# Three edits to a fused sparse-attention and expert kernel: the gate's weight by a transfer, one joint set of block sums, an uneven last output

## The chip, the cores and the metric

The kernel runs on one core of a Trainium2 chip. The metric is device time in microseconds of one execution; the time before is the median of three runs, 151.57 us (151.08 to 153.88). A trace from the hardware profiler covers one further execution.

## What is computed

Four batches, 8 heads, 768 positions, head size 64. Each query attends to keys less than 16 positions away and to 24 block summaries of its head (the maximum of 32 keys, the mean of 32 values, plus log 32 on the score). The heads side by side give `x` of 768 x 512 per batch. The mean of `x` over the positions times a 512 x 8 matrix picks one of 8 experts per batch and a weight, and that expert's two products follow.

```python
scores = concat([where(|i - j| < 16, q k^T / 8, -1e9), q k_sum^T / 8 + log(32)])
x = softmax(scores) @ concat([v, v_sum])              # 4 x 768 x 512
logits = x.mean(positions) @ w_gate                   # 4 x 8
e, g = argmax(logits), max(softmax(logits))           # one expert and one weight per batch
out[b] = g * (relu(x[b] @ w1[e]) @ w2[e])             # 512 -> 1024 -> 512
```

## The kernel before, in words

Work is tiled by batch `b` (0 to 3), by pair of heads `pr` (0 to 3) and by parity `u` of the 64-query tile. For a pair, TensorE (PE) turns the keys (`tk`, L555) and the queries (`tq`, L602); VectorE (DVE) and ScalarE (ACT) move them out of PSUM (`ke` and `ko`, two window copies of the keys; `eq` for the queries; all at L412 or L414), DVE takes the maximum per block of keys (`kmw`, L579) and ACT copies it in beside the windows (`kb`, L588). Then come the scores (`qk`, L624; in batch 0 with two products of a mask more, L634), the exponential on ACT (`ex`, L643 or L646), a mask on DVE (`mk`, L652, batches 1 to 3), the product with the values (`av`, L671 and L682), the division on DVE (`nm`, L694 and L695), a transpose (`tx`, L708) and a copy to `xT` on ACT, which also sums over the positions (`xc`, L716).

The values need block sums (`v_ops`): products of the values with a 0/1 matrix. For batches 0 and 1 each half of the heads has a set of 7 products over all 128 output rows (`half`, L435). For batches 2 and 3 one set of 14 products does both halves, each product using 64 columns of the array at its own place (`joint`, L461). Their results are copied by `ev` and spread to the tiles `vb` and `vo` by DVE (`sums`, L490; `odd`, L509 and L511).

The gate of a batch (`gate`): `lgf` (L857), four fp32 products of the sums with `w_gate`; `mxf` (L864 to L869), the maximum and its index on DVE; `ldf`, GpSimd (POOL) reads the index into a register and sends for the chosen expert's weights, `w1` (L882; for batch 0 in three parts of 256, 256 and 512 columns) and `w2` (L888). On the side, `exf` (ACT, L895) and `rcf` (DVE, L902) make the weight g in one element; `gpf` (PE, L905) multiplies it with a row of ones, which brings it to 128 partitions of a PSUM bank, and `gcf` (DVE, L912) copies that to `gcol`. In batch 0 the last pair's sum comes from `pxf` (PE, L843) and `pcf` (DVE, L849).

The expert (`moe`): `h` (L960), products with `w1` into one PSUM bank each, 12 groups a batch, with `rl` (ACT L971 or DVE L973) after each; then six row blocks `o_st` (L996, 8 products of 512 columns), `ev` (ACT L1005 or DVE L1007), which scales by `gcol`, and an output transfer on SyncE's (SP's) queue (L1013). An output tile is one of 7 buffers. The last block of the last batch is made in two pieces of 256 columns.

Nothing is reordered while it runs. Each piece of work is added once with a number, and `ORDER` (L21) is the order in which all are issued; `ENGINE` says which of DVE or ACT does a copy; `FILL` puts idle products (L1152, 128 x 512, results unused) ahead of a numbered piece on PE. Each engine's queue takes its pieces in that order and waits at the first that isn't ready. POOL's queue, in order: the loads of q, k, v of batches 0 and 1; gate 0's `w1`, half of batch 2's q and k, `w2`, the rest of batch 2; gate 1's `w1`, batch 3's loads with `w2` of batch 1 between them; then `w1`, `w2` of gates 2 and 3. PSUM holds one double bank (`pair`), five single banks and the two banks of `kps` for turned keys. Setup work of DVE (masks, memsets; `setup_far`, L282, `setup_bind`, L304) is in the same order.

The three stages the text speaks of: the start (0 to 30 us, batch 0's attention, ended by gate 0), the middle (30 to 90 us, attention of batches 1 and 2 mixed with the experts of 0 and 1) and the end (batch 3's attention, the experts of 2 and 3).

Of the kernel before, what the change touches and what calls it, by code (L numbers as in the profile page):

```python
# [10 lines left out]
FP32 = mybir.dt.float32  # L11
# [4 lines left out]
ACT = mybir.ActivationFunctionType  # L16
# [2 lines left out]


ORDER = [  # L21
    2, 5, 4, 21, 23, 25, 0, 1, 3, 8, 6, 11, 12, 13, 7, 22, 24, 34, 14, 35, 36, 41, 9, 10, 39,
    29, 27, 46, 42, 37, 40, 38, 55, 47, 15, 43, 56, 44, 45, 57, 30, 61, 16, 26, 17, 28, 18,
    19, 20, 31, 48, 58, 32, 59, 33, 49, 62, 60, 50, 63, 65, 51, 53, 69, 74, 54, 75, 76, 77,
    66, 52, 70, 71, 72, 78, 80, 82, 86, 79, 88, 73, 106, 83, 87, 92, 90, 93, 64, 96, 67, 89,
    94, 137, 100, 97, 81, 91, 95, 68, 138, 102, 107, 108, 139, 84, 98, 101, 85, 147, 103, 112,
    99, 142, 148, 149, 140, 113, 109, 114, 130, 115, 125, 121, 143, 141, 164, 152, 110, 111,
    116, 117, 118, 119, 122, 123, 144, 126, 165, 166, 154, 150, 124, 104, 145, 183, 129, 169,
    167, 153, 131, 151, 159, 155, 168, 170, 188, 127, 160, 171, 178, 189, 105, 146, 132, 128,
    157, 325, 134, 172, 179, 321, 213, 156, 214, 326, 161, 162, 176, 190, 184, 329, 173, 163,  # L30
    323, 158, 177, 322, 185, 330, 327, 133, 333, 191, 324, 135, 174, 343, 335, 186, 334, 181,
    180, 238, 192, 136, 175, 344, 195, 328, 187, 197, 202, 336, 337, 182, 198, 239, 203, 199,
    196, 341, 342, 339, 204, 240, 338, 248, 200, 120, 340, 201, 243, 207, 209, 253, 244, 208,
    205, 210, 254, 206, 331, 193, 241, 211, 194, 212, 249, 332, 345, 219, 242, 215, 250, 346,
    245, 220, 255, 348, 224, 246, 216, 351, 251, 265, 225, 252, 226, 256, 349, 231, 230, 257,
    266, 267, 260, 272, 227, 247, 352, 268, 261, 273, 354, 217, 218, 284, 270, 269, 289, 221,
    228, 271, 285, 290, 229, 232, 237, 279, 280, 355, 286, 357, 358, 360, 361, 222, 468, 262,
    474, 469, 475, 314, 234, 315, 316, 317, 223, 274, 235, 233, 318, 319, 460, 458, 258, 236,
    263, 461, 277, 282, 459, 382, 387, 291, 287, 288, 264, 259, 383, 278, 384, 388, 281, 292,
    320, 480, 466, 481, 467, 283, 298, 303, 299, 304, 392, 296, 393, 478, 464, 385, 479, 465,  # L40
    472, 473, 275, 297, 476, 394, 300, 470, 386, 477, 471, 276, 305, 293, 301, 395, 409, 308,
    310, 374, 302, 311, 389, 390, 391, 462, 306, 309, 350, 347, 359, 410, 307, 294, 411, 375,
    295, 482, 356, 312, 463, 485, 483, 313, 363, 353, 412, 413, 364, 486, 397, 414, 398, 428,
    415, 396, 372, 373, 433, 368, 399, 404, 434, 369, 488, 400, 405, 376, 377, 379, 406, 370,
    371, 429, 430, 401, 489, 416, 423, 417, 418, 424, 431, 491, 402, 407, 492, 408, 403, 421,
    426, 422, 435, 494, 436, 425, 432, 442, 447, 443, 448, 497, 378, 427, 495, 365, 419, 420,
    366, 367, 438, 439, 381, 437, 527, 380, 515, 509, 517, 498, 449, 444, 516, 510, 528, 518,
    440, 445, 446, 452, 454, 455, 523, 529, 524, 525, 441, 493, 450, 453, 456, 511, 451, 530,
    531, 457, 500, 512, 521, 526, 532, 496, 487, 362, 519, 484, 501, 505, 522, 490, 520, 502,
    513, 499, 533, 534, 536, 537, 514, 539, 542, 506, 507, 545, 508, 548, 540, 543, 503, 571,  # L50
    504, 572, 567, 546, 568, 538, 569, 563, 564, 559, 549, 565, 557, 566, 558, 560, 553, 573,
    574, 554, 570, 551, 561, 555, 552, 556, 575, 578, 541, 581, 562, 576, 535, 547, 579, 550,
    580, 544, 584, 582, 583, 585, 586, 577, 587, 590, 588, 591, 589, 593, 594, 592, 595,
]

ENGINE = {
    7: "DVE", 8: "ACT", 9: "ACT", 10: "DVE", 31: "ACT", 35: "DVE", 36: "ACT", 40: "DVE", 42:
    "ACT", 43: "ACT", 47: "DVE", 49: "DVE", 50: "ACT", 54: "DVE", 70: "ACT", 71: "ACT", 75:
    "DVE", 87: "DVE", 126: "ACT", 128: "ACT", 138: "ACT", 139: "ACT", 143: "DVE", 148: "ACT",
    149: "ACT", 153: "DVE", 165: "ACT", 166: "ACT", 170: "DVE", 184: "ACT", 185: "ACT", 189:  # L60
    "DVE", 229: "DVE", 239: "DVE", 240: "ACT", 244: "ACT", 249: "DVE", 250: "ACT", 254: "ACT",
    266: "ACT", 267: "ACT", 271: "ACT", 285: "DVE", 286: "ACT", 290: "DVE", 322: "ACT", 324:
    "ACT", 326: "ACT", 328: "DVE", 330: "ACT", 332: "DVE", 334: "ACT", 336: "ACT", 338: "ACT",
    340: "ACT", 342: "DVE", 344: "ACT", 346: "ACT", 349: "ACT", 352: "DVE", 355: "ACT", 358:
    "ACT", 361: "ACT", 373: "ACT", 383: "ACT", 384: "ACT", 388: "DVE", 393: "DVE", 394: "ACT",
    398: "ACT", 410: "ACT", 411: "DVE", 415: "DVE", 429: "ACT", 430: "ACT", 434: "DVE", 459:
    "ACT", 461: "ACT", 463: "DVE", 465: "ACT", 467: "ACT", 469: "ACT", 471: "ACT", 473: "ACT",
    475: "ACT", 477: "ACT", 479: "ACT", 481: "ACT", 483: "ACT", 486: "DVE", 489: "DVE", 492:
    "ACT", 495: "ACT", 498: "ACT", 510: "ACT", 512: "ACT", 514: "ACT", 516: "ACT", 518: "ACT",
    520: "DVE", 522: "ACT", 524: "ACT", 526: "DVE", 528: "DVE", 530: "DVE", 532: "ACT", 534:  # L70
    "DVE", 537: "ACT", 540: "DVE", 543: "ACT", 546: "DVE", 549: "DVE", 552: "DVE", 554: "DVE",
    556: "DVE", 558: "ACT", 560: "DVE", 562: "DVE", 564: "ACT", 566: "DVE", 568: "DVE", 570:
    "ACT", 572: "DVE", 574: "ACT", 576: "DVE", 579: "ACT", 582: "ACT", 585: "ACT", 588: "DVE",
    591: "ACT", 594: "ACT",
}

FILL = {
    34: 11, 41: 6, 46: 2, 55: 1, 98: 1, 104: 1, 144: 1, 154: 1, 164: 1,
}


# [79 lines left out]
def kernel(  # L161
# [10 lines left out]
    nc = tc.nc  # L172

    B, H, S, D = q.shape
    E = moe_w_gate.shape[1]
    DM = H * D
# [12 lines left out]
    NST = S // 128  # L189
# [3 lines left out]
    SP = S // G  # L193
# [12 lines left out]
    const_pool = ctx.enter_context(tc.tile_pool(name="const", bufs=1))  # L206
# [36 lines left out]

    BIND = 4 * (NT - 1)
    bind = const_pool.tile([128, BIND + 128], BF16, name="bind")
    ones_row = const_pool.tile([1, 128], FP32, name="ones_row")

# [64 lines left out]
            nc.vector.memset(kps.bitcast(FP32)[:, :, a // 2 : (a + PADA) // 2], 0.0)  # L314

    def setup_kw():
        nc.vector.memset(ones_row, 1.0)
        for t in kws:
            nc.vector.memset(t[:, :, :, KW + NB : 128], 0.0)

# [68 lines left out]
        nc.gpsimd.dma_start(wg_sb, moe_w_gate.rearrange("(g p) e -> p g e", p=128))  # L389

    sch = Sched(len(single))
    JOINT = 2
    add = sch.add
    state = {}
    last_T, last_av = {}, {}
# [439 lines left out]
    def gate(b, att, w_deps, order, between=None):  # L835
        sb = state[b]
        _, x_ops, x_sums = att
        last = by_pe(b, NP - 1)
# [62 lines left out]
            sb["grec"] = sm_pool.tile([1, 1], FP32, name="grec")  # L901
            nc.vector.reciprocal(sb["grec"], sb["se"])  # L902

        def gpf():
            nc.tensor.matmul(  # L905
                sb["lgps"][:, E : E + 1], lhsT=ones_row[0:1, :], rhs=sb["grec"][0:1, 0:1],
                start=True, stop=True,
            )

        def gcf():  # L910
            sb["gcol"] = sm_pool.tile([128, 1], FP32, name="gcol", bufs=B)
            nc.vector.tensor_copy(sb["gcol"], sb["lgps"][:, E : E + 1])  # L912

        if last:
            o_px = add("PE", 0.35, x_sums, pxf, num=12, shape="w", take=1)
            o_pc = add("DVE", 0.16, [o_px, x_ops[0]], pcf)
            o_lg = add("PE", 0.2, x_ops[:-1] + [o_pc, wg_load], lgf, num=8, shape="w")
        else:
            o_px = o_lg = add("PE", 0.2, x_ops + [wg_load], lgf, num=8, shape="w", take=1)
        o_mx = add("DVE", 0.67, [o_lg], mxf)  # L920
        o_ld = add("POOL", 1.5, [o_mx] + w_deps, ldf, after=order)
        w1s, prev, c0 = [], [o_ld], 0
        for c1 in W1_PARTS[b]:
# [8 lines left out]
        w2 = add("POOL", 0.9, [], w2f, dma=6.2, count=1, after=prev)  # L932
        o_ex = add("ACT", 0.3, [o_mx], exf)
        o_rc = add("DVE", 0.15, [o_ex], rcf)
        o_gp = add("PE", 0.3, [o_rc, kw_set], gpf, num=2, shape="g")
        o_gc = add("DVE", 0.16, [o_gp], gcf, give=[o_px])
        return w1s, w2, o_gc

    EVICT = 20.0
# [1 line left out]
    def moe(b, w, att):  # L941
        w1s, w2, o_gc = w
        sb = state[b]
# [92 lines left out]
        hsl["first"] = firsts[0]  # L1036
        last = [o_st(st) for st in range(NST - (b == B - 1))]
        if b == B - 1:
            last += [o_st(NST - 1, 0, DM // 2), o_st(NST - 1, DM // 2, DM)]
        return last  # L1040


# [84 lines left out]
    order = load_batch(1, order)  # L1127
    sch.prio = 60.0
    gates[0] = gate(0, att[0], [], order)
    order = [gates[0][2]]  # L1130
    att[1] = attend(1, 30.0)
    order = load_batch(2, order)
    sch.prio = 30.0
    gates[1] = gate(1, att[1], [], order)
    order = [gates[1][2]]
    for b in range(B):
        if b + 2 < B:
            att[b + 2] = attend(b + 2, 10.0)
            if b + 3 < B:
                sch.prio = 0.0  # L1140
                order = load_batch(b + 3, order)
        sch.prio = 0.0
        moe_last[b] = moe(b, gates[b], att[b])
        if b + 2 < B:
            sch.prio = 10.0
            gates[b + 2] = gate(b + 2, att[b + 2], moe_last[b], order)
            order = [gates[b + 2][2]]

    def fill(i, n):

# [37 lines left out]
```

## Time and profile before

| | |
|---|---|
| median of 3 runs | 151.57 us |
| the profiled execution, its own time | 152.49 us |
| span of its trace | 150.7 us |
| busy: PE, DVE, ACT, POOL | 141.6, 103.8, 94.0, 35.2 us |
| mean granted TensorE clock | 0.989 |
| software DMA queue (POOL's): moved, share of 16 engines' span | 17.50 MB, 94.3% |
| hardware DMA queue (SP's): moved, share | 7.08 MB, 13.3% |

Times in the trace count from the start of the span; 1.8 us of the execution lie outside it. In a timeline row stand start, length, engine, line, operation, output and inputs, count, and in brackets the idle time before it with what ended it ("issue" is idle time for which the profile shows no wait). In the slices each digit is a fortieth of the span (3.77 us) in tenths. Of a transfer the trace gives the time from issue to landing.

### The profile page before, as it was taken

The numbers are of one execution on the slowest core, as the hardware profiler recorded it, in microseconds if no ns is written. First come the engines' busy times: TensorE is split into PE (matmuls) and PEld (weight loads), VectorE is DVE, ScalarE is ACT, GpSimd is POOL, SyncE is SP. The second block draws the span as 40 slices with busy tenths as digits, with TensorE's granted clock in tenths as the row PEclk, the third lists the DMA queues.
The fourth block names the chain that finished last, engine by engine and source line by source line (L and its number), as shares of the span: only waits on it lengthen the run. The fifth ranks groups of instructions, "written<-read, shape, count | busy, mean of one in ns | idle before, by whom it ended". The sixth has DMA issues, their size and how long they took to land.

```text
span 150.7 us, 4728 instructions
## 1 busy us (share of the span) xinstructions
PE 141.6 (94%) x2005; PEld 87.4 (58%) x2023; DVE 103.8 (69%) x244; ACT 94.0 (62%) x185; POOL 35.2 (23%) x44
## 2 busy tenths in 40 slices
PE   6988989799999999999899999999999999999990
PEld 2356758567657665566564857555576445465460
DVE  5988987569999889589579978999453222556010
ACT  3277877769968899776788978969563310140331
POOL 7959500039900004942000005000004000000000
PEclk9999999879999999999999999999999999999999
DMA  4999999919999999999999991999931999910353
GB/s 147 190 171 185 190 177 195 123 11 146 166 207 202 174 197 118 145 246 218 251 215 207 192 71 11 184 157 232 353 121 5 174 146 243 299 41 0 129 222 140
DMA packets 42565, 24.88 MB, mean 165 GB/s; under 512 B 26016, under 2 KB 37680, under 8 KB 42544
## 3 DMA queue, kind: packets, MB, share of 16 engines
q0 software_dynamic: 38528, 17.50, 94.3%
q1 hardware_dynamic: 4016, 7.08, 13.3%
q8 instruction: 16, 0.26, 0.7%
q14 instruction: 5, 0.04, 0.1%
HBM read 35.77 MB, written 6.29 MB: 279 GB/s over the span
## 4 chain that ended last, share of the span: by engine, by line
PE 71%; DVE 10%; DMA 10%; issue 5%; ACT 1%; POOL 1%; POOLq 0%; ACTq 0%
PE one L960 26%; PE one L996 22%; DMA q_nat<-in_q_dram 10%; PE one L671 4%; PE one L708 3%; PE one L602 3%; PE kps L555 3%; PE pair L624 2%; PE one L435 2%; DVE kmx L579 1%; PE one L682 1%; PE one L624 1%; DVE far L286 1%; DVE vo L511 1%; DVE qT L414 1%
## 5 line engine op out<-in xcount | busy, mean ns | idle before, releaser
L960 PE MATMUL one<-xT_b,w_sb 128*128 128x256 bf16 (+1 forms) x247 | 43.5, 324 | 0.5
L996 PE MATMUL one<-w_sb,hT_sb 128*128 128x512 bf16 (+1 forms) x191 | 42.8, 370 | 0.7 <-issue 0.3
L960 PEld LDWEIGHTS <-w_sb 128*128 128x128 bf16 x256 | 24.2, 98 | 15.1 <-DMA w_sb<-in_moe_w_dram 0.2
L996 PEld LDWEIGHTS <-hT_sb 128*128 128x128 bf16 x200 | 18.7, 98 | 19.5
L971 ACT ACTIVATE hT_sb<-one 128x512 bf16<-128x512 f32 x32 | 19.0, 600 | 15.0 <-PE one L960 8.2
L882 POOL DMA_DIRECT2D w_sb<-in_moe_w_dram x6 | 4.6, 764 | 75.6 <-PE one L461 22.2
L1005 ACT ACTIVATE o_sb<-one,gcol 128x512 f32<-128x512 f32 (+1 forms) x16 | 10.6, 661 | 18.0 <-issue 9.7
L412 ACT ACTIVATE kw<-kps 128x576 bf16<-128x576 bf16 x25 | 15.6, 655 | 5.5 <-DVE kw L414 3.2
L695 DVE TENSOR_TENSOR xs<-one,rv 128x384 bf16<-128x384 f32 x32 | 17.8, 558 | 1.1
L643 ACT ACTIVATE aT<-pair 128x768 bf16<-128x768 f32 x19 | 15.4, 810 | 3.4 <-PE pair L624 1.9
L973 DVE TENSOR_SCALAR hT_sb<-one 128x512 bf16<-128x512 f32 x16 | 10.7, 686 | 9.3 <-PE one L960 9.2
L579 DVE TENSOR_REDUCE kmx<-kw 128x24 bf16<-128x768 bf16 x16 | 15.1, 945 | 0.5 <-ACT kw L412 0.3
L716 ACT ACTIVATE xT_b<-one 128x768 bf16<-128x768 bf16 x16 | 12.8, 806 | 1.9 <-PE one L708 1.7
L652 DVE TENSOR_TENSOR aT<-aT,keep 128x768 bf16<-128x768 bf16 x24 | 12.8, 554 | 0.5 <-ACT aT L643 0.2
L1007 DVE TENSOR_SCALAR o_sb<-one,gcol 128x512 f32<-128x512 f32 x9 | 6.7, 744 | 8.4 <-PE one L996 8.4
L646 ACT ACTIVATE aT<-one 128x384 bf16<-128x384 f32 x26 | 11.3, 491 | 1.6 <-PE one L624 1.0
L374 POOL DMA_DIRECT2D vb<-in_v_dram x8 | 12.1, 1511 | 0.0
L671 PEld LDWEIGHTS <-aT 120*64 120x64 bf16 (+1 forms) x384 | 7.9, 111 | 4.1 <-issue 3.1
L1152 PE MATMUL one<-idle_in 128*128 128x512 bf16 x25 | 9.1, 482 | 1.2 <-DVE warm L251 1.2
L602 PE MATMUL one<-identb,q_nat 96*64 96x96 bf16 x256 | 8.4, 211 | 1.5 <-issue 1.1
L624 PEld LDWEIGHTS <-kw 64*128 64x128 bf16 x384 | 7.0, 95 | 4.3 <-issue 2.2
L694 DVE RECIPROCAL rv<-one 128x6 f32<-128x6 f32 x32 | 6.0, 187 | 4.6 <-PE one L671 3.8
(85 smaller groups left out, 167.0 us busy)
## 6 DMA issues: line engine op xcount, KB each, us to landing
w_sb<-in_moe_w_dram POOLq DMA_DIRECT2D x7, 1024.0 KB, 15.5
out_dram<-o_sb SPq DMA_DIRECT2D x23, 256.0 KB, 5.9
k_nat<-in_k_dram POOLq DMA_DIRECT2D x6, 384.0 KB, 13.1
q_nat<-in_q_dram POOLq DMA_DIRECT2D x6, 384.0 KB, 14.6
vb<-in_v_dram POOLq DMA_DIRECT2D x4, 384.0 KB, 14.0
vb<-in_v_dram POOLq DMA_DIRECT2D x3, 400.0 KB, 17.8
k_nat<-in_k_dram POOLq DMA_DIRECT2D x3, 192.0 KB, 7.1
q_nat<-in_q_dram POOLq DMA_DIRECT2D x3, 192.0 KB, 7.3
```

The costliest lines, as they stand in the source:

```text
L374: nc.gpsimd.dma_start(vbs[b % 2][:, n0 + skip : n0 + n, 0:D], tokens[t0 + 128 * skip : t0 + 128 * n].rearrange("(s p) d -> p s d", p=128),)
L412: nc.scalar.activation(dst, src, ACT.Copy)
L579: nc.vector.tensor_reduce(out=sb["km"][pr].rearrange("p (j n) -> p j n", n=QB // BLK), in_=sb["kT"][pr][:, :, :, HALO : HALO + QB].rearran ...
L602: nc.tensor.transpose(qps[hh * D : (hh + 1) * D, :, g, :], qk_nat[b][0][:, 2 * pr + hh, g, :], identb[0:SP, 0:SP],)
L643: nc.scalar.activation(aT, pair[:, :, 0 : NI * QB], ACT.Exp, scale=SCALE)
L652: nc.vector.tensor_tensor(out=aT, in0=aT, in1=keeps[u].rearrange("p i c -> p (i c)").unsqueeze(1).to_broadcast([128, 2, NI * QB]), op=ALU. ...
L671: nc.tensor.matmul(ops[c0 : c0 + QB, hh, i // 2, :], lhsT=aT[rows, hh, i * QB : (i + 1) * QB], rhs=(vo if u else vb)[rows, PT * (2 * pr + ...
L695: nc.vector.tensor_tensor(out=sb["xs"][pr][:, u * 3 : u * 3 + 3, :, :].rearrange("p s h d -> p h s d"), in0=ops[:, :, :, 0:D], in1=rv.unsq ...
L716: nc.scalar.activation(sb["xT"][:, pr, :].rearrange("p (j e g) -> p j e g", e=QB // G, g=G), sb["xps"][pr].rearrange("p j g e -> p j e g") ...
L960: nc.tensor.matmul(ps["t"][:, i * n : (i + 1) * n], lhsT=sb["w1"][:, dt, ft * 128 : (ft + 1) * 128], rhs=sb["xT"][:, dt, c0:c1], start=(dt ...
L971: nc.scalar.activation(dst, src, ACT.Relu)
L996: nc.tensor.matmul(ps["t"][:, 0 : c1 - c0], lhsT=sb["hT"][:, ft, st * 128 : (st + 1) * 128], rhs=sb["w2"][:, ft, c0:c1], start=(ft == 0), ...
```

## The change

- `gpf` and the row of ones go. `gcf` is now a transfer on SP's queue that reads the one element 128 times and writes 128 partitions of 4 bytes. The PSUM bank of the gate is given back after `mxf`. The loads behind a gate now name, as what they follow, the last `w1` transfer in place of `gcf`.
- Batch 1's block sums take the joint form (`JOINT` from 2 to 1).
- The last row block is made in 384 and 128 columns.
- `ORDER`, `ENGINE` and `FILL` are written anew for the changed list of pieces (590 in place of 596).

```diff
-    2, 5, 4, 21, 23, 25, 0, 1, 3, 8, 6, 11, 12, 13, 7, 22, 24, 34, 14, 35, 36, 41, 9, 10, 39,
...
+    0, 28, 2, 8, 21, 5, 22, 1, 10, 4, 11, 3, 9, 6, 23, 7, 25, 34, 35, 12, 39, 40, 36, 41, 37,
...
 FILL = {
-    34: 11, 41: 6, 46: 2, 55: 1, 98: 1, 104: 1, 144: 1, 154: 1, 164: 1,
+    34: 10, 39: 6, 46: 2, 55: 1, 57: 1, 86: 1, 114: 1, 144: 1, 161: 1, 166: 3,
 }
...
-    JOINT = 2
+    JOINT = 1
...
-        def gpf():
-            nc.tensor.matmul(
-                sb["lgps"][:, E : E + 1], lhsT=ones_row[0:1, :], rhs=sb["grec"][0:1, 0:1],
-                start=True, stop=True,
-            )
-
         def gcf():
             sb["gcol"] = sm_pool.tile([128, 1], FP32, name="gcol", bufs=B)
-            nc.vector.tensor_copy(sb["gcol"], sb["lgps"][:, E : E + 1])
+            one = sb["grec"][0:1, 0:1]
+            nc.sync.dma_start(sb["gcol"], bass.AP(one.tensor, one.offset, [one.ap[0], [0, 128], [1, 1]]))
...
-        o_mx = add("DVE", 0.67, [o_lg], mxf)
+        o_mx = add("DVE", 0.67, [o_lg], mxf, give=[o_px])
...
-        o_gp = add("PE", 0.3, [o_rc, kw_set], gpf, num=2, shape="g")
-        o_gc = add("DVE", 0.16, [o_gp], gcf, give=[o_px])
+        o_gc = add("SP", 0.45, [o_rc], gcf, dma=0.3)
...
-            last += [o_st(NST - 1, 0, DM // 2), o_st(NST - 1, DM // 2, DM)]
+            last += [o_st(NST - 1, 0, 3 * DM // 4), o_st(NST - 1, 3 * DM // 4, DM)]
```

What the new order does on each engine, where the steps below touch it:

- DVE, ahead of the first key copy: a memset of `vo`, `setup_band`, a memset of `vb`, `setup_far` of u = 0, the other `vb`, `setup_kps`, `setup_ident`, `setup_far` of u = 1. Before: two `vb`, `setup_band`, `setup_far` of u = 1, the row of ones and three memsets of `kw`, `setup_kps`, `setup_ident`.
- Up to gate 0, DVE takes four window copies of keys more and one copy of block sums more, ACT three copies of queries and one of the first queries more.
- PE at gate 0: before `tk` (batch 1, pair 1), `pxf`, `tq` (batch 1, pair 0), `lgf`; now one idle product, `tk`, `pxf`, one idle product, `lgf`, `tq`.
- PE after gate 0, up to the first products with columns 512 to 1023 of batch 0's `w1`: before they stand behind four groups of `h` with a fifth ([0,1], [0], [3], [1], [2]); now behind [0,1], [1], [0], [2,3], [2]; batch 1's second `half`, and all of `gpf`, are gone from this stretch.
- PE in batch 3: the query transpose of pair 0 stands 11 places later, and the transposes `tx` (batch 2, pair 3) and `tq` (batch 3, pair 1) come ahead of the first row block of batch 1, where they stood behind it.
- SP: `gcf` of batch 0 is first of all, `gcf` of batch 1 stands ahead of five of batch 0's outputs, `gcf` of batch 2 ahead of batch 2's outputs, `gcf` of batch 3 ahead of the last output of batch 1.
- POOL's queue is the same, instruction by instruction.

## The prediction

> **What bounds the kernel now.** I read the page's slices first, then the waits and issues of the transfers, then the timeline around each place where PE stood still.
>
> ```profile
> PE   6988989799999999999899999999999999999990
> DVE  5988987569999889589579978999453222556010
> PEclk9999999879999999999999999999999999999999
> DMA  4999999919999999999999991999931999910353
> ```
>
> PE is full from slice 10 to 39, so at first sight only PE work counts. But the DMA row is full as well, from slice 9 to 23 (34 to 90 us), with a hole ahead of it. The hole is gate 0:
>
> ```profile
> 27.61 0.28 PE L602 MATMUL one<-identb,q_nat 96*64 96x96 bf16 x4
> 28.97 0.69 PE L602 MATMUL one<-identb,q_nat 96*64 96x96 bf16 x12 [1.09 <-issue]
> 29.59 0.35 PE L857 MATMUL one<-wg_sb,pooled 128*1 128x8 f32 x8
> ...
> 32.43 2.25 POOL L882 DMA_DIRECT2D w_sb<-in_moe_w_dram  x3 [15.26 <-DVE kmx L579]
> ```
>
> The routing product (`lgf`, L857) stands behind a query transpose that stopped for 1.09 us; the weights are sent for 2.5 us after it. From then on the queue never empties: gate 1's loads go out at 58.6 us, while batch 2's last load (issued 39.77, 21.3 us to landing) lands at 61.1. So all loads up to 90 us hang on gate 0's time. PE meets that stream in three places:
>
> ```profile
> 43.74 0.62 PEld L960 LDWEIGHTS <-w_sb 128*128 128x128 bf16 x4 [0.24 <-DMA w_sb<-in_moe_w_dram]
> ...
> 74.59 0.53 PE L602 MATMUL one<-identb,q_nat 96*64 96x96 bf16 x16 [0.43 <-DMA q_nat<-in_q_dram]
> ...
> 85.91 1.89 PE L996 MATMUL one<-w_sb,hT_sb 128*128 128x512 bf16 x7
> ```
>
> The first needs the third part of batch 0's `w1`, the second batch 3's queries. The third, batch 1's first row block, waits for nothing but is only just late enough for its `w2`. From the issues of transfers (two windows):
>
> ```profile
> w_sb<-in_moe_w_dram POOLq DMA_DIRECT2D x1, 512.0 KB, 9.8
> ...
> w_sb<-in_moe_w_dram POOLq DMA_DIRECT2D x1, 1024.0 KB, 22.6
> ```
>
> The first row: issue 33.9 + 9.8 = 43.7 us. The second: 62.9 + 22.6 = 85.5 us, 0.4 ahead of 85.91. After 86 us only PE counts: 61.3 us of products to 147.2.
>
> **The change, part by part.** Baseline: the profiled execution, 152.49 us, of which 150.7 are the span. The median of the runs is 0.92 lower; I take differences in the span and subtract them from the median.
>
> *Gate 0, by the new order (start, 0 to 30 us).* `lgf` moves ahead of the query transpose: 29.59 - 27.61 = 2.0 us of PE queue are gone from before it, so it can start when its sums are there. What is late next? VectorE. Its work up to batch 0's last division changes by four window copies more (4 x 0.75), one copy of block sums more (0.42), three query copies less (3 x 0.5), one first cast less (0.5), the ones' memset less (0.17): +1.25 us. The new list also puts `setup_far` and memsets ahead of the first key cast; by the sum of the rows that cast starts at about 6.0 us instead of 5.17, but the later copies then follow with fewer setups between, and batch 0's first scores come out near 10.0 us against 10.5. Against the 1.25 stand some 0.7 us of idle VectorE before 24.57 that a busier engine fills. I take the last division to end 0.5 late (27.4 for 26.9; bounds -0.2 to +1.3), then `kmw` 0.94, `pcf` 0.16, so `lgf` could end at 28.85, 1.0 us sooner than 29.87.
>
> [...] First, two setup operations on DVE are not priced by their size:
>
> ```profile
> 2.97 1.43 POOL L374 DMA_DIRECT2D vb<-in_v_dram  x1
> ...
> 3.34 1.07 DVE L286 TENSOR_SCALAR far<-band 16x64 bf16<-16x64 bf16 x1
> ```
>
> 64 elements a row take 1.07 us and end as POOL's issue does (4.40), while 384 elements take 0.27 elsewhere. [...] I use the row: the cast at 6.0 has it in.
>
> Second, the 1.09 us stop. In the built program the two stops of PE marked "issue" (0.74 at 22.03 and this one) come after 704 and 960 rows, 256 apart, and the "instruction" queue moved 16 packets of 16 KB. [...] In the new program row 960 falls inside `lgf` itself. [...] I take -0.4, bounds -1.4 (idle gone as well) to +2.1 (all of VectorE's 1.25 and the 0.85 of the later cast unhidden).
>
> *Batch 1's joint sums.* 14 products of 256 columns before, in two sets of 0.78 us at full clock (the first took 1.6 at half clock); the joint form in batches 2 and 3 did 14 in 0.78: -0.78 on PE, one PSUM copy of 0.4 less. `gpf`: two pieces of 0.16, 0.31 us a gate with their weights. But the sums and batch 0's `gpf` lie in 30 to 43 us, where PE runs into the third part of `w1`: the first part lands at about 36.2 (issue 32.0 + 4.2), then five groups of `h` (4.4), two `av` and two `qk` (0.9) bring PE there at 41.5, 1.8 us early. Cover: that transfer; cost on the path 0; without the cover 1.1 us gained. So `w1`'s third part lands at 43.3, and PE starts the following stretch then.
>
> *43.3 to batch 1's first row block.* Before: 43.83 to 85.91 = 42.1 us. Differences of the two queues: one `av` more (0.19), one `qk` less (0.28), `gpf` of batch 1 less (0.31), one `tx` and one `tq` more (0.34 each), the wait at 74.59 gone because that transpose stands 11 places later (about 0.5): -0.2. PE is there at 43.3 + 41.9 = 85.2. The `w2` it needs: 85.5 - 0.4 = 85.1; but one output more (batch 0's sixth) is sent before it, 13.3% of 150.7 us for 7.08 MB, so 0.7 us per 256 KB, bounds 0 and 0.7; I take 0.35: 85.45. The transfer decides: -0.45 against 85.91.
>
> *After it.* The `tx` and `tq` already done: -0.68. `gpf` of batches 2 and 3: -0.62. All other products are the same. -1.3.
>
> *The gate's weight by a transfer.* DVE loses four copies of 0.16, hidden. `gcf` waits on SP for `rcf`. Batch 0's `rcf` comes after batch 1's last masks, about 49 us; the scaling that needs it is at about 55.5. No row shows a transfer of 4-byte pieces. The nearest by packets are the outputs: 1.8 us with the queue idle at the end, 8.3 at 60 to 64 us beside a full queue. Kept at 8.3 it comes 2 us after ACT wants it, at 1.8 it is hidden by 4.5; I take 0, since PE arrives 0.25 before `w2` and ACT has 2.6 to 2.9 us of work in each 4 us of this stretch; both ends stay in the range. Queued behind batch 1's `gcf` are five of batch 0's outputs, now sent at about 73 instead of 60 to 70. With 7 output tiles, the first who waits for one of them is batch 1's eviction at about 88. Batch 3's `gcf` has 15 us to spare. Gates 2 and 3 hold up only later outputs.
>
> *Last output.* 384 and 128 columns: the last eviction is a quarter of a 512-column one on DVE (0.75 / 4 plus overhead, about 0.3) in place of 0.47, and 64 KB in place of 128; the first piece's longer eviction (0.58) and SP's issues eat some of it. -0.15, bounds -0.4 and +0.2.
>
> Sum: -0.45 - 1.3 - 0.15 = -1.9 us. Span 148.8, profiled execution 150.6, median 151.57 - 1.9 = **149.7 us**.
>
> **The rivals.**
>
> *The start gains more.* The stop falls elsewhere, or the PE clock holds. The windows show what the idle cost:
>
> ```profile
> 27.00:29.00 2.00, 0.91 (x28) 0.73 (x30) 1.42 (x3) 2.00 (x6) 0.00 (x0) 0.98 2.13 147
> 29.00:31.00 2.00, 2.00 (x26) 1.53 (x26) 0.96 (x6) 0.58 (x4) 0.00 (x0) 0.50 0.56 43
> 31.00:33.00 2.00, 2.00 (x37) 1.25 (x36) 1.09 (x3) 1.05 (x4) 0.57 (x1) 0.67 0.07 5
> ```
>
> With 0.91 of 2 us busy, the granted clock is halved for the next 3.3 us (2 at 0.50, then 2 at 0.67). For: idle products now stand on both sides of `lgf`. [...] Gate 0 at -1.4 and no extra output cost: -1.8 - 1.3 - 0.15, 148.3 us.
>
> *VectorE becomes the bound in the middle.* It is busy 25 of 32 us from 56 to 88. The new assignment gives it three window copies (2.25), three `rl` (2.1) and one query copy more, less two `mk` and `odd`: about +3.6, 29 of 32 in a fixed order. If PE waits 1.5 us more for divisions, or ACT as long for batch 0's `gcol`, the rest is -0.4: 151.2 us, no change.
>
> *Slower: VectorE's start isn't recovered.* Place: DVE from 3 to 27 us. Price: gate 0 late by x makes everything up to 86 us late by x; the rest of the sum, -1.45 and 0.35 for the output, is -1.1. It decides from x = 1.1, `lgf` ending after 31.0 us. At +2.1: 152.6 us. For: DVE has only 1.5 us of idle between 15 and 27 us. Against: two of its stalls behind POOL may go.
>
> *The parts do nothing:* the removed PE work lies before waits for transfers and the later part's too. Against: PE is 99% busy after 86 us with no wait for transfers. 151.1 us, in the second case.
>
> **How the numbers follow.** Likeliest (the sum): 0.50, with its own range 148.6 to 150.9. More gain: 0.17. VectorE or a wait eats it, or the parts do nothing: 0.19. Slower: 0.14. Two per cent, about what a measurement of this kernel can tell from no change, is 3.0 us: 148.5 and 154.6. Faster takes two thirds of the second case and a little of the first: 0.14. Slower by 2% takes half of the last case, where gate 0's delay meets another such half-clock stretch (1.6 us), and 0.02 for what isn't named: 0.09. Within: 0.77. Range with no more than 2 in 10 outside: 147.9 to 152.9.
>
> **What would show it.** Right: `lgf` (now L855) ends at 29 to 30 us with a stop of about 1 us inside or beside it; `w1`'s first issue near 32; DMA row full to about 89; first row block of batch 1 at 85 to 86 with a short wait for `w_sb`; PE's end near 145.3. Wrong: gate 0 after 31; PE waiting for VectorE (`xs`, `aT`) in 56 to 88; ACT waiting for a transfer to `gcol`; a second stretch with a granted clock of 0.5.

## The result and the profile after

| | before | after |
|---|---|---|
| median, measured side by side (4 runs each) | 152.72 us (151.08 to 155.23) | 149.19 us (149.02 to 149.35) |
| ratio, 95% interval | | 0.9859 [0.9824, 0.9893] |
| the profiled execution, its span | 152.49, 150.7 us | 149.09, 147.3 us |
| mean granted TensorE clock | 0.989 | 1.000 |

The ratio leaves out runs in which the chip was disturbed, so it is nearer to 1 than the quotient of the medians. It says 1.4% faster, about 2.1 us. The spans differ by 3.4 us, mostly because the profiled execution of the kernel before was itself 1.2 us above the 151.3 that the ratio has for that kernel. Differences to the kernel before that are read from the traces below have this in them.

The slices of the kernel after, to be held against those of before:

```profile
PE   6999989899899998999999999999999999999990
DVE  4898978699999787899995987979822422310220
PEclk9999999999999999999999999999999999999999
DMA  4999999989999999999999945999801999930153
```

Two things are gone. The hole in the DMA row at slice 8 (a 1) is now an 8, so the weights of gate 0 were sent almost before the stream ran dry; and the two slices of PEclk under 9 are gone in this execution. In a second trace of the same kernel the granted clock was 0.56 and 0.58 from 28 to 32 us, and batch 1's first row block came only 0.15 us later (84.23), so the change alone does not decide the clock there, and little hangs on it. In exchange the stream has a new thin place in slices 23 and 24 (85 to 92 us), so the transfers were done there before PE was.

PE at gate 0 in the kernel after, and the issue of the weights that it sets off (POOL):

```profile
27.01 0.17 PE L855 MATMUL one<-wg_sb,pooled 128*1 128x8 f32 x1
27.77 0.32 PE L855 MATMUL one<-wg_sb,pooled 128*1 128x8 f32 x7 [0.58 <-issue]
...
30.57 2.25 POOL L880 DMA_DIRECT2D w_sb<-in_moe_w_dram  x3 [12.72 <-DVE vo L507]
```

The routing product starts at 27.01, stops inside itself after one of its eight products, goes on at 27.77 and ends at 28.09. Before, it ended at 29.94. The weights leave at 30.57 instead of 32.43.

Batch 1's first row block, and the `w2` that the forecast made it wait for:

```profile
84.08 1.89 PE L988 MATMUL one<-w_sb,hT_sb 128*128 128x512 bf16 x8
```
```profile
w_sb<-in_moe_w_dram POOLq DMA_DIRECT2D x1, 1024.0 KB, 19.8
```

The row block begins at 84.08 (before 85.91), without a wait. Its `w2`, issued at 60.23, landed at 80.0 (before: 62.9 + 22.6 = 85.5), four microseconds early. From the row block to PE's end 59.92 us pass (before 61.32), and from there to the end of the span 3.3 (before 3.47).

### The profile page after: what moved, and what is told of

The parts are those of the page before. It is cut to its first block, busy times and chain, and to the rows that moved or that the text cites. A ratio compares the mean times of both kernels' runs of the same rounds, so it can differ in the third digit from the quotient of the medians.

```text
span 147.3 us, 4743 instructions
## 1 busy us (share of the span) xinstructions
PE 139.6 (95%) x2017; PEld 84.8 (58%) x2017; DVE 100.4 (68%) x238; ACT 95.5 (65%) x187; POOL 35.1 (24%) x44
## 4 chain that ended last, share of the span: by engine, by line
PE 65%; DMA 17%; DVE 12%; issue 2%; ACT 2%; POOL 0%; POOLq 0%; DVEq 0%; ACTq 0%
PE one L988 26%; PE one L952 22%; DMA vb<-in_v_dram 8%; DMA gcol<-grec 5%; DMA k_nat<-in_k_dram 4%; PE one L669 3%; DVE kmx L577 3%; PE one L600 3%; PE one L706 2%; DVE xs L693 2%; PE pair L622 2%; PE kps L553 2%; DVE aT L650 2%; PE one L459 2%; PE one L622 1%
## 5 line engine op out<-in xcount | busy, mean ns | idle before, releaser
L952 PE MATMUL one<-xT_b,w_sb 128*128 128x512 bf16 (+1 forms) x256 | 44.6, 326 | 0.3 <-DMA w_sb<-in_moe_w_dram 0.3
L988 PE MATMUL one<-w_sb,hT_sb 128*128 128x512 bf16 (+2 forms) x200 | 43.2, 371 | 0.0
L963 ACT ACTIVATE hT_sb<-one 128x512 bf16<-128x512 f32 x38 | 22.0, 600 | 10.8 <-PE one L952 10.7
L999 DVE TENSOR_SCALAR o_sb<-one,gcol 128x512 f32<-128x512 f32 (+1 forms) x9 | 6.3, 704 | 18.3 <-PE one L988 17.2
L641 ACT ACTIVATE aT<-pair 128x768 bf16<-128x768 f32 x17 | 13.8, 812 | 4.5 <-PE pair L622 3.1
L644 ACT ACTIVATE aT<-one 128x384 bf16<-128x384 f32 x30 | 13.1, 494 | 0.8 <-PE one L632 0.8
L965 DVE TENSOR_SCALAR hT_sb<-one 128x512 bf16<-128x512 f32 x10 | 6.9, 686 | 8.7 <-PE one L952 8.6
L410 ACT ACTIVATE kw<-kps 128x576 bf16<-128x576 bf16 x18 | 11.2, 652 | 1.6 <-PE kps L553 1.3
L412 DVE COPY kw<-kps 128x576 bf16<-128x576 bf16 x14 | 10.1, 748 | 0.9 <-PE kps L553 0.9
```

The lines of the kernel that those rows point to most:

```text
L641: nc.scalar.activation(aT, pair[:, :, 0 : NI * QB], ACT.Exp, scale=SCALE)
L644: nc.scalar.activation(aT[:, hh, :], single[banks[hh]][:, 0 : NI * QB], ACT.Exp, scale=SCALE)
L952: nc.tensor.matmul(ps["t"][:, i * n : (i + 1) * n], lhsT=sb["w1"][:, dt, ft * 128 : (ft + 1) * 128], rhs=sb["xT"][:, dt, c0:c1], start=(dt ...
L963: nc.scalar.activation(dst, src, ACT.Relu)
L988: nc.tensor.matmul(ps["t"][:, 0 : c1 - c0], lhsT=sb["hT"][:, ft, st * 128 : (st + 1) * 128], rhs=sb["w2"][:, ft, c0:c1], start=(ft == 0), ...
```

## The experiments

Theory going in: the start (0 to 30 us, VectorE's earlier division and the place of the routing product) brings what was not forecast; the removed `gpf` and the moved transposes bring what was. Each is tried alone. Times are medians; "the kernel after" is 149.19 us, and 149.15 (148.84 to 150.18) repeated on another chip. The experiments ran on three chips, and only three of them (the early transfer, the early outputs, the equal pieces) on the same one as a run of the kernel after. In the times that the ratios have for the kernel before, these chips differ by up to 0.3 us, so a difference of that size between chips says nothing.

### The start alone

The kernel before with the new order, engines and idle products up to the routing product, and its own order after that; then the reverse, the kernel after with the old start.

```diff
 ORDER = [
-    2, 5, 4, 21, 23, 25, 0, 1, 3, 8, 6, 11, 12, 13, 7, 22, 24, 34, 14, 35, 36, 41, 9, 10, 39,
+    0, 28, 2, 8, 21, 5, 22, 1, 10, 4, 11, 3, 9, 6, 23, 7, 25, 34, 35, 12, 39, 40, 36, 41, 37,
...
-    112, 99, 142, 148, 149, 140, 113, 109, 114, 130, 115,
+    112, 113, 149, 114, 142, 130, 115,
```

> The kernel before, with the changed kernel's order, engines and idle products for everything up to gate 0's routing product (the start), and its own order for all that follows; none of the three edits. If the time won ahead of batch 1's first row block comes from gate 0 ending sooner: gate 0 near 28.1 us in place of 29.9, the transfers follow, time 1.4 to 1.9 us under the kernel before (about 150). If it comes from the edits or from the later order: no change (151.6).

Measured: 150.41 us (12 runs), ratio to before 0.994 [0.9889, 0.9991]: 0.9 us, less than the 1.4 to 1.9 expected. In its trace gate 0 ends at 27.95 and batch 1's first row block begins at 83.76, 2.15 sooner than in the trace of before; the traced execution of before was 1.2 us above its kernel's time, about the gap to 0.9.

> The mirror: the changed kernel with the old order of the start. If gate 0's time sets the middle: gate 0 again near 29.9 us, batch 1's first row block at 85.5 to 86, time 150.7 to 151.1. If the edits and the later order carry the gain: 149.2 to 149.5.

Measured: 150.86 us (12 runs), ratio 0.9959 [0.9912, 1.0005]. PE at gate 0 with the old start in the kernel after:

```profile
28.73 0.60 PE L597 MATMUL one<-identb,q_nat 96*64 96x96 bf16 x12 [1.09 <-issue]
29.26 0.34 PE L852 MATMUL one<-wg_sb,pooled 128*1 128x8 f32 x8
```

The stop of 1.09 is back, and the product ends at 29.60. Batch 1's first row block begins at 86.52, later than the 85.5 to 86 expected: this execution was granted a clock of 0.5 from 29 to 35 us. So the start is worth 0.6%, 0.9 us, in the old kernel and 1.5 (by the two ratios) to 1.7 (150.86 - 149.19) in the new one; of the 2.1 in all that leaves 0.4 to 1.2 for the rest of the change. The theory holds in that gate 0 and the time move together in both kernels; the sizes are shares of one path and need not add up the same way in both.

### The place of the routing product alone

The kernel before with the product ahead of the query transpose, and the kernel after with it (and the idle product ahead of it) behind. Shown is the first of the two edits.

```diff
-    112, 99, 142, 148, 149, 140, 113, 109, 114, 130,
+    112, 99, 148, 149, 140, 113, 109, 114, 142, 130,
```

> The kernel before, and batch 0's routing product put ahead of the query transpose of batch 1's first pair; nothing else is moved. Theory (the start's gain is a sum of two parts: VectorE's earlier last division, about 0.9 us, and the product's place): the sums are there at 27.9 as before, PE's stop at row 960 now falls inside the product and lasts to about 29.0 as before, so the product ends near 29.3 instead of 29.94: 0.6 us gained, and the first row block of batch 1 near 85.3. Rival (the place alone does it): the product ends near 28.2, 1.7 us gained, as with the whole new start. Rival (the place does nothing, the stop decides all): 29.9, the time of before.

Measured: 151.85 us (13 runs) beside 151.90, ratio 0.9993 [0.995, 1.0037]. The gain of 1.7 is excluded, that of 0.6 (0.996) just not. Its profiled execution was granted a clock of 0.5 from about 24 to 41 us, so its trace settles nothing: whether the place gave 0 or 0.6 in the old kernel stays open.

> The kernel after, and batch 0's routing product put back behind the query transpose of batch 1's first pair. Theory of two parts: VectorE's division ends at 26.0 as in the kernel after, the stop at row 960 falls inside the transpose and ends at about 27.8, the product ends 0.46 later than 28.09, near 28.55; everything after follows: about 149.6 us, 0.45 above the kernel after. Rival (the place is the whole of the start's gain): product end near 29.7, 150.8 us. Rival (the place counts nothing): 149.2.

Measured: 150.10 us (12 runs), ratio 0.9902 [0.9865, 0.9938]. PE, from the transpose to the second part of batch 0's `w1`:

```profile
27.08 0.27 PE L597 MATMUL one<-identb,q_nat 96*64 96x96 bf16 x3
27.50 0.48 PE L597 MATMUL one<-identb,q_nat 96*64 96x96 bf16 x13 [0.15 <-issue]
...
28.24 0.35 PE L852 MATMUL one<-wg_sb,pooled 128*1 128x8 f32 x8
...
38.75 1.91 PE L949 MATMUL one<-xT_b,w_sb 128*128 128x256 bf16 x12 [0.98 <-DMA w_sb<-in_moe_w_dram]
```

The product ended at 28.59, as expected (28.55), 0.50 later than in the kernel after. The time rose by 0.9, not 0.45: the wait for the weights at 38.75 took 0.98 where the kernel after has none at that place. But 28.59 does not measure what the place is worth. In the ten traces that have this start with the product ahead of the transpose, it ends anywhere from 27.67 to 28.55, and the run with the early transfer, below, has it at 28.55 without that wait and is 1.4 us faster than this one.

### The weight by a product again

The kernel after, with a product of the one element and a row of ones in a bank of its own, and VectorE's copy, in place of the transfer. Then the same product with its result unused, its bank free at once, and the transfer kept.

```diff
-            one = sb["grec"][0:1, 0:1]
-            nc.sync.dma_start(sb["gcol"], bass.AP(one.tensor, one.offset, [one.ap[0], [0, 128], [1, 1]]))
+            nc.vector.tensor_copy(sb["gcol"], sb["gps"][:, E : E + 1])
...
-        o_gc = add("SP", 0.45, [o_rc], gcf, dma=0.3)
+        o_gp = add("PE", 0.3, [o_rc, kw_set], gpf, num=2, shape="g", take=1)
+        o_gc = add("DVE", 0.16, [o_gp], gcf, give=[o_gp])
```

> The changed kernel with the gate's weight by a product again (a bank of its own, at the place in the order where the transfer stood), copied by VectorE. By the sum on record the products of batches 2 and 3 count in full, those of 0 and 1 don't, and ScalarE's wait for batch 0's weight goes: +0.2 to +0.7, 149.4 to 149.9. If every removed product counts: +1.3, 150.5. If the transfer's wait cost more than the products: under 149.0.

Measured: 151.39 us (151.09 to 153.08, 12 runs), 2.2 above the kernel after: neither number. PE at the second and third gate:

```profile
82.91 0.38 PE L904 MATMUL one<-grec,ones_row 1*128 1x1 f32 x2
83.53 0.49 PE L706 MATMUL one<-identb,xs 128*128 128x128 bf16 x6 [0.25 <-DVE gcol L911]
...
120.49 0.38 PE L904 MATMUL one<-grec,ones_row 1*128 1x1 f32 x2
121.11 3.61 PE L995 MATMUL one<-w_sb,hT_sb 128*128 128x512 bf16 x16 [0.25 <-DVE gcol L911]
```

PE stands still for VectorE's copy: the next user of a bank got the one that the copy had to empty, and it comes 0.62 after the product instead of 0.31. A bank given back late had not been in the expectation.

> The kernel after, with the gates' product of one element and a row of ones done as well, into a bank that is free again at once, its result unused; the weight still comes by the transfer. Tells the product's own time from the wait for its bank. Theory (of the 2.2 us that the product with its copy cost in the kernel after, about 0.31 a gate is PE's own time, and the rest is the next user of its bank waiting for the copy, twice 0.31, and gate 0's share is covered by the wait for the transfer): 3 x 0.31 = 0.9 above the kernel after, 150.1 us. Rival (the product itself costs it all, by what it does to the array's rhythm): 151.4. Rival (the place of the stops in the first 35 us made it): 149.2 to 149.5.

Measured: 150.45 us (150.04 to 150.84, 12 runs), 1.25 above the kernel after. PE at the third gate:

```profile
120.48 0.38 PE L903 MATMUL one<-grec,ones_row 1*128 1x1 f32 x2
120.79 3.63 PE L996 MATMUL one<-w_sb,hT_sb 128*128 128x512 bf16 x16
```

The wait for the bank is gone; the product is still there, and the stretch around each is 0.41 us longer than in the kernel after, not 0.31 (batch 2's first row block to the first `h` of batch 3: 113.48 to 124.25 here, 10.77 us, for 10.36 there; 10.78 in the kernel before). Gate 0's was not covered either: from the first products with the third part of batch 0's `w1` to batch 0's first row block PE took 10.84 for 10.42. So the product costs 4 x 0.4 in this order, 1.6 at PE's end (145.60 for 144.00). The wait for its bank costs 0.74 more over the second and third gate (0.85 - 0.41 and 0.71 - 0.41, the same stretches of the two runs). With the transfer's wait of about 0.5 gone, which the next run shows, that makes 1.9 for the run with the copy, as its PE has it (145.92). The times, 1.25 and 2.2, come from three chips and bear this out only roughly.

### The transfer earlier

The kernel after, with batch 0's `exf`, `rcf` and `gcf` ahead of a score exponential of batch 1, so that the transfer leaves sooner.

```diff
-    187, 194, 188, 121,
+    187, 194, 121, 122, 123, 188,
```

> The changed kernel with batch 0's weight made sooner: its exponential one place earlier on ScalarE, its reciprocal and transfer right behind it, so that the transfer leaves at about 42 us in place of 47.6. If ScalarE's wait of 1.6 us for it is on the path: the stop of 0.5 us on TensorE at 56.2 goes, 148.6 to 148.8. If transfers set the middle all the same: 149.2.

Measured: 148.69 us (148.42 to 148.87, 6 runs), ratio 0.9818 [0.9778, 0.9857], against 149.15 on the same chip. First SP, ACT and PE in the kernel after, then SP, ACT and PE here:

```profile
47.60 0.54 SPq L905 DMA_DIRECT2D gcol<-grec  x1
...
54.62 0.69 ACT L997 ACTIVATE o_sb<-one,gcol 128x512 f32<-128x512 f32 x1 [1.57 <-DMA gcol<-grec]
...
56.18 0.35 PE L622 MATMUL pair<-qT,kw 64*128 64x64 bf16 x12 [0.53 <-ACT kw L586]
```
```profile
43.87 0.54 SPq L902 DMA_DIRECT2D gcol<-grec  x1
...
54.03 0.69 ACT L994 ACTIVATE o_sb<-one,gcol 128x512 f32<-128x512 f32 x1 [0.52 <-PE one L985]
...
56.04 0.35 PE L619 MATMUL pair<-qT,kw 64*128 64x64 bf16 x12
```

In the kernel after, ACT reached the first scaling at 53.05 and stood 1.57 us for 512 bytes that had been 6.9 us under way; the copy of the key maxima (L586) queued behind it came late, and PE lost 0.53. Sent 3.7 us sooner, all of that is gone, and the time with it (0.46). In this trace gate 0 had ended 0.46 later than in the kernel after, and PE began batch 0's first row block as much later (52.11 for 51.65); it is ahead from 56 us on.

### Batch 0's outputs earlier, the sums in halves, the last block in equal pieces

Three edits to the kernel after: gate 1's transfer behind five of batch 0's outputs on SP's queue instead of ahead of them; batch 1's sums in two sets; 256 and 256 columns.

```diff
-    223, 352, 349,
+    352, 349,
...
+    223, 391, 394,
```
```diff
-    JOINT = 1
+    JOINT = 2
```
```diff
-            last += [o_st(NST - 1, 0, 3 * DM // 4), o_st(NST - 1, 3 * DM // 4, DM)]
+            last += [o_st(NST - 1, 0, DM // 2), o_st(NST - 1, DM // 2, DM)]
```

> The changed kernel with batch 1's weight transfer behind batch 0's outputs on SyncE's queue, so that five outputs leave at 57 to 68 us in place of 73 and later. If holding them back is what brought batch 1's second weights in at 80.0 in place of 85.5: they land 2 to 4 us later (82 to 84), and with the first row block at 84.1 the time stays within 0.3 of 149.2. If the middle hangs on that landing: +0.5 or more.

Measured: 148.93 us (148.30 to 150.21, 6 runs), within the kernel after. But the transfer did move; `w2` of batch 1 here, issued at 60.04:

```profile
w_sb<-in_moe_w_dram POOLq DMA_DIRECT2D x1, 1024.0 KB, 24.1
```

24.1 us to landing instead of 19.8: five outputs in its way are worth 4.3 us between these two traces, and it lands at 84.1, just as its products come up (84.18). In the other traces with the outputs held back it took 19.4 to 21.4, and 23.4 in the joined version with the outputs early, so the worth is 2.0 to 4.7.

> The changed kernel with batch 1's block sums in two sets of products again. By the sum on record the 0.78 us lie ahead of the wait for the expert's first weights and cost nothing: 149.1 to 149.4. If TensorE's work counts there: 150.0.

Measured: 149.76 us (148.91 to 152.12, 6 runs). Two of the six, at 151.51 and 152.12, were granted a clock of 0.977; the other four have a median of 149.16, the time of the kernel after. The trace (profiled at 148.91) agrees: PE on the sums, in halves and then jointly in the kernel after.

```profile
33.75 1.72 PE L432 MATMUL one<-vb,bind 128*128 128x256 bf16 x14
```
```profile
33.32 0.97 PE L459 MATMUL one<-vb,bind 128*64 128x256 bf16 x14
```

0.75 us more, and the first `h` 0.7 later (35.69 for 34.98; a stop of 0.78 marked "issue" at 32.94 is in that too), yet gate 1's product begins at 53.41 for 53.47 and batch 1's first row block at 83.98 for 84.08. The wait of 0.67 for the sums, at 40.46 in the kernel after, takes it up (that trace has no such wait).

> The changed kernel with the last row block in two pieces of 256 columns again. By the sum on record +0.15 (149.35), bounds -0.2 and +0.4.

Measured: 149.41 us (149.09 to 151.53) beside 149.15 (148.84 to 150.18): the sign expected, but the ranges overlap, so 0.15 is not shown by the times. VectorE's last eviction took 0.48 with 256 columns and 0.35 with 128, but from PE's end to the end of the span 3.3 us pass in both traces (144.41 to 147.7; 144.00 to 147.3). What the uneven block is worth is not shown, and may be nothing.

### A version that joins what was found

Early transfer, early outputs, and VectorE's copy of the block sums ahead of the fourth pair's key maximum.

```diff
-    183, 327, 130, 328, 184, 129,
+    327, 130, 328, 129, 183, 184,
...
-    187, 194, 188, 121,
+    187, 121, 122, 123, 188,
...
+    331, 194,
```

> The kernel after, with batch 0's weight computed and sent early and batch 0's row-block outputs as in the two runs before, and in batch 1's attention VectorE's copy of the block sums put ahead of the fourth pair's key maximum (with the score products that need that maximum one group of expert products later). The wait of PE for the sums at 40.9 (0.78) should go, and what follows on PE moves with it. If PE's queue is what sets the time from 40 us on: 0.46 for the transfer and about 0.7 for the sums, 148.0 us. If VectorE's queue is as late as PE there, or the changed order of the banks brings a wait: 148.7, what the early transfer alone gave.

Measured: 148.61 us (147.51 to 149.59, 6 runs), ratio 0.9781 [0.9721, 0.9841]. It beats both kernels, but not the early transfer alone (148.69). PE there:

```profile
41.66 0.33 PE L619 MATMUL one<-qT,kw 64*128 64x64 bf16 x11 [0.18 <-ACT hT_sb L960]
42.33 1.90 PE L949 MATMUL one<-xT_b,w_sb 128*128 128x512 bf16 x12 [0.34 <-DVE xs L690]
```

The wait of 0.78 for the sums is gone, and two others stand a microsecond later, 0.18 for ScalarE and 0.34 for VectorE. So the move won 0.26 in this place, and two thirds of what was left is VectorE again, as the second theory had it.

## Why the forecast was right, and which step of it was not

The time fell within the forecast's range, 0.5 us under the forecast value. That it fell so near is luck: in the spans of the two traces the change is worth 3.4 us (the last three rows below) where the sum had 1.9. The forecast took its differences from a traced execution that lay 1.2 us above what the kernel before takes, and subtracted them from a median that does not.

The steps, in microseconds of the span:

| step | forecast | measured |
|---|---|---|
| end of gate 0's product | -0.4 | -1.85 |
| batch 1's first row block | -0.45 | -1.83 |
| from there to PE's end | -1.3 | -1.40 |
| after PE's end | -0.15 | -0.17 |

**The step that failed** is the end of gate 0, and in it VectorE's start: "I take the last division to end 0.5 late (27.4 for 26.9)". It ended at 26.04. The division in the kernel before, in the kernel after, and in the run with the early transfer:

```profile
26.36 0.56 DVE L695 TENSOR_TENSOR xs<-one,rv 128x384 bf16<-128x384 f32 x1
```
```profile
25.48 0.56 DVE L693 TENSOR_TENSOR xs<-one,rv 128x384 bf16<-128x384 f32 x1
```
```profile
26.28 0.56 DVE L690 TENSOR_TENSOR xs<-one,rv 128x384 bf16<-128x384 f32 x1
```

The list of copies was right (four window copies came to 2.97 us more, block sums 0.41, query copies 1.63 less). But I had priced one instruction held up by POOL and left two others in the sum as if they were the work's own length; that "two of its stalls behind POOL may go" stood only under the rival "Slower". From the timeline before, VectorE's two instructions and POOL's issues in which they lie:

```profile
7.59 1.43 POOL L374 DMA_DIRECT2D vb<-in_v_dram  x1
...
8.40 0.71 DVE L300 TENSOR_SCALAR keep<-far 128x384 bf16<-128x384 bf16 x1
...
12.66 1.73 POOL L374 DMA_DIRECT2D vb<-in_v_dram  x1
...
13.24 1.50 DVE L511 COPY vo<-vb 32x1536 bf16<-32x1536 bf16 x1
```

and VectorE's timeline after:

```profile
3.11 0.26 DVE L285 TENSOR_SCALAR far<-band 128x384 bf16<-128x384 bf16 x1
...
3.98 0.47 DVE L269 TENSOR_SCALAR identb<-diff 128x128 bf16<-128x128 f32 x1
...
4.76 0.21 DVE L285 TENSOR_SCALAR far<-band 16x64 bf16<-16x64 bf16 x1
5.00 0.42 DVE L412 CAST k_nat<-first 96x512 bf16<-96x512 f32 x1
...
12.06 0.55 DVE L509 COPY vo<-vb 32x1536 bf16<-32x1536 bf16 x1
...
22.32 0.43 DVE L299 TENSOR_SCALAR keep<-far 128x384 bf16<-128x384 bf16 x2
```

In the kernel after the same three instructions (1.07, 0.71 and 1.50 us before) lie outside POOL's long `vb` issues and take 0.21, 0.22 and 0.55. That is 2.3 less, against 0.4 more for two setups that now overlap POOL's issue at 3 to 4.4. VectorE's busy time from 2.6 us to the last division fell from 21.44 to 20.24 us where I had +1.25. And the key cast began at 5.00, not 6.0: the moved `setup_far`, which I had ending with POOL's issue as in the row of before, ran from 3.11 to 3.37, and the issue ended at 4.41 (next section but one).

Only part of this belongs to the order. Eleven traces have this start. In all of them the setup and the mask (`keep`) are short. But in five of them one of the first two `vo` copies meets the `vb` issue again, as in the run with the early transfer (POOL, then VectorE):

```profile
12.83 1.56 POOL L369 DMA_DIRECT2D vb<-in_v_dram  x1
...
13.26 1.51 DVE L504 COPY vo<-vb 64x1536 bf16<-64x1536 bf16 x1
```

In these five the last division ends at 26.43 to 26.84, in the other six at 25.52 to 26.04. So about 0.8 us of VectorE's lead in the kernel after is chance: its second copy began at 12.64, 0.2 ahead of the issue. The forecast's 27.4 came in none.

VectorE's lead does not set gate 0 by itself either. PE on the routing product in the second trace of the kernel after, where the last division ended at 25.52, and in the run with the early transfer, where it ended at 26.84:

```profile
26.50 0.17 PE L855 MATMUL one<-wg_sb,pooled 128*1 128x8 f32 x1
27.73 0.32 PE L855 MATMUL one<-wg_sb,pooled 128*1 128x8 f32 x7 [1.06 <-issue]
```
```profile
27.82 0.17 PE L852 MATMUL one<-wg_sb,pooled 128*1 128x8 f32 x1
28.23 0.32 PE L852 MATMUL one<-wg_sb,pooled 128*1 128x8 f32 x7 [0.25 <-issue]
```

A division 0.52 sooner than in the first trace of the kernel after left the product's end where it was (28.05 for 28.09), because PE's stop grew from 0.58 to 1.06. And with a division only 0.08 sooner than in the kernel before the product still ended at 28.55, 1.39 sooner. Counted from the stop, the -1.85 is a stop that ends 1.20 sooner (27.77 for 28.97), and 0.65 for the place: 0.32 of PE's work follows the stop where 0.97 did. What brought the stop's end forward stays open: no run parts VectorE's lead, the transposes that follow it and the transfer on the "instruction" queue (next point).

**The stop of PE** was right in kind: it fell inside the product. From the transpose `tx` of pair 2 to the stop's end 2.46 us passed (25.31 to 27.77), about as in the trace of before (2.49, 26.48 to 28.97). But that was no fixed time: in the seven traces of this start with the stop inside the product it is 2.0 to 2.9, for instance 2.93 in the second trace of the kernel after (`tx` at 24.80) and 2.12 with the early transfer (26.11), so that the 2.46 agrees by chance. In both traces the "instruction" queue began to move a packet of 16 KB about when that transpose began, at 26.45 before (1.01 us long) and at 25.39 after (0.97), 2.52 and 2.38 us ahead of the stop's end. Whether PE waited for it, no run shows. Nor does a run show the -0.4 that the sum has for gate 0, my estimate of how far this stop would move: measured was -1.85, and over the ten traces of this start with the product ahead of the transpose an end at 27.67 to 28.55 for the 29.94 of before.

**The middle.** With gate 0 at -1.85, `w1`'s third part landed at 40.1 instead of the forecast 43.3 (issue 1.4 sooner, 8.0 us to landing instead of 9.8). The cover for batch 1's sums was then no longer that transfer but the 0.67 us wait for VectorE's copy; the price 0 held (the run with halves). "The transfer decides" failed: I booked +0.35 for one more output ahead of `w2`, while the new order holds five outputs back to 73.2 us, as the forecast itself said two paragraphs on, and that is worth -2.0 to -4.7 (the run with early outputs). That error is masked: PE was not there before 84.08, so both gave the same time. From 41.23 to 84.08 PE took 42.85 us where I had 41.9; 0.53 of the difference is the next point, the other 0.4 I cannot assign to a row.

**The transfer of the weight** was costed at nothing, with 8.3 us as the bad end. It took 6.9 in batch 0 (2.3 to 6.9 over the four), and the cover I named, that PE comes early, didn't hide it: the price was 0.46 (shown by the early transfer). "PE ahead of `w2`" was no cover, as `w2` was early. "ACT waiting for a transfer to `gcol`", which the forecast named as a sign of being wrong, is what the trace shows.

**After the row block**: two transposes moved ahead 0.68, two products gone. Those cost 0.31 (94.62 to 94.93 in the kernel before) and 0.41 (in a run of `h`), together 0.72 for the forecast 0.62; the sum is 1.40, as measured. The -0.17 after PE's end cannot be put down to the uneven block (the run with equal pieces).

**The rivals.** Start gains more: its gate 0 beyond -1.4 came true, and in the spans so did its sum (3.25 forecast, 3.4 measured). The half-clock stretch was gone in the first trace and back in the second (0.56 and 0.58). Its whole time, 148.3, did not come: the transfer took 0.5 back and the trace of before had been 1.2 us too long. VectorE as a bound in the middle: PE's waits of the kernel after from 42 to 147 us hold only the 0.53. Slower: excluded by gate 0 at 28.09.

## What to carry to other kernels

When an order is changed, price each instruction of the old trace that is longer than its like elsewhere (here 1.07, 0.71 and 1.50 us for 0.21, 0.22 and 0.55) as a stall, not as work: ask whether the new order still meets what held it, and whether it does so in every execution: a second trace of the same kernel tells. Time won ahead of a wait on another cause, here PE's stop, can be lost in that wait (0.52 us of VectorE's here). A small transfer that replaces a product and a copy is not free when its reader stands in a queue with others behind it (0.46 us here); its latency beside a full stream (6.9 us here) is what to compare with the slack. A product of one element can cost twice its own time if its bank is given back by another engine (0.62 us for 0.31 here).

## What the runs showed of the hardware

When VectorE was held by POOL, it was to nearly one moment: a TENSOR_SCALAR or COPY between bf16 tiles in SBUF that started 0.37 us or more inside a long `vb` issue (1.43 to 1.73 us) ended as if it had run its own length from 0.13 to 0.20 us before the issue's end (0.13 is the second setup in the kernel after, 4.54 - 0.26 = 4.28 for an issue that ends at 4.41; keep: 9.11 - 0.25 = 8.86 for an issue that ends at 9.02; the `vo` copy: 14.74 - 0.55 = 14.19 for 14.39). Two more in the kernel after, from the timeline of VectorE and POOL:

```profile
35.12 1.54 POOL L372 DMA_DIRECT2D vb<-in_v_dram  x1
...
36.07 0.97 DVE L509 COPY vo<-vb 32x1536 bf16<-32x1536 bf16 x1
...
37.99 1.46 POOL L372 DMA_DIRECT2D vb<-in_v_dram  x1
...
38.76 1.08 DVE L507 COPY vo<-vb 64x1536 bf16<-64x1536 bf16 x1
```

37.04 - 0.55 is 0.17 before 36.66, and 39.84 - 0.56 is 0.17 before 39.45. Two that started within 0.15 us of the issue's start were not held: `setup_far` at 3.11 (issue from 2.96) took 0.26, and with the old start in the kernel after, `keep` at 8.26 (issue from 8.12) took 0.26; in the kernel before, at 8.40, 0.81 into its issue, it took 0.71. The earliest start that was held is 0.37 into the issue (3.34 for 2.97). Two copies out of PSUM were not held (13.46, both in 1.40, under the issue from 12.85 to 14.41). Nor were two other operations on bf16 tiles in SBUF, in the kernel before: a mask (TENSOR_TENSOR) at 37.50, 0.61 into the issue from 36.89, took 0.56, and a key maximum (TENSOR_REDUCE) at 16.25, 0.51 into the issue from 15.74, took 0.95. What in the chip sets these apart, no run shows.
